# POOL's subtraction of the expert weights cut in four, and a longer allowance for one phase of the routing search

## The chip, the cores and the metric

The kernel runs on one core of a Trainium2 chip. The metric is the device time of one execution in microseconds (us). A core has a matrix engine (PE, TensorE), a vector engine (DVE, VectorE), an activation engine (ACT, ScalarE), a general engine (POOL, GpSimd) and a queue engine (SP) that only issues transfers here. Each engine works through its own list of instructions in order and waits on semaphores for the others.

## The reference

Three layers follow one another, all in float32. Local attention works on chunks of 64 tokens in 8 heads. Its 4608 rows of 512 go through a dense feed-forward layer, `relu(x @ w_in)**2 @ w_out` with 2048 hidden columns. The last layer routes each row to one of 8 experts, and it is the layer of which this document speaks:

```python
logits = x @ w_gate
order = np.argsort(-logits.flatten())
for idx in order:
    tok, e = idx // E, idx % E
    if assigned[tok] >= 0 or counts[e] >= cap:
        continue
    assigned[tok] = e
    counts[e] += 1
...
h = np.maximum(x[mask] @ w1[e], 0.0)
out[mask] = h @ w2[e]
```

Each expert takes exactly `cap` = 576 rows, those that the greedy pass over all 36864 logits gives it.

## The kernel before

**Products.** A float32 matrix is held as a high part, the value rounded to the narrower format that PE multiplies, and a low part, what is left. A product is three matmuls: high by high, high by low, low by high. ACT copies the high part (`WH`, line 920 for expert weights) and another engine subtracts it from the value to get the low part (`WL`, line 921, on POOL, `wl<-raw,wh` in the rows: 128 partitions by 512 columns).

**The greedy pass as a search.** The experts fill up one after another. Phase `ph` (0 to 7) of the search finds the expert that fills next, its threshold and its list of rows. It works on DVE with small matmuls on PE between (`route_phase`). A phase has a start of four steps (lines 700 to 713: `M`, `b`, `wq`, `ch`, `oh`, `mk`), eight rounds that fix four bits of the threshold each, and an end that gives the expert's number (`EID`, line 813) and then the list (`idx`, line 876). A round has a chain from PE to DVE and back: counts on PE (line 733), DVE, a second small matmul (lines 741 and 760 in phases 0 and 1, line 753 from phase 2 on, behind DVE's `c<-all,c` of line 750), DVE's digit and the next thresholds (`thr` line 782, `base` line 784, `mk` line 725, `pre` line 728). Phase 7 has no rounds.

**The experts.** The loop at the end takes the experts `p` = 0 to 7 in the order in which the search finds them. For each of eight slices `f` of the hidden columns it does `up2(p, f)` (192 matmuls in all, line 1007) and, one slice behind, `down2` (112 matmuls, line 1072). Both `down2(p, 6)` and `down2(p, 7)` come at `f` = 7, and between their matmuls PE transposes the five tiles of rows of expert `p+1` (line 985), at places that `SPREAD` fixes. These tiles are fetched by indirect DMAs that POOL issues (`gather`, line 970). They are issued after `up2(p, f)`, as many as are due so that five are done at `f` = 7, but only once the list of `p+1` exists. At `f` = 7 what is missing of the search is put out without delay and what is missing of the five gathers is issued at once. POOL also issues the indirect DMAs that write results (`put`, line 1057).

**What sets the order.** Every engine's list is made by one Python program, with a clock of its own that runs on estimated costs: `tick` adds 0.12 us for a matmul of `up2` and 0.216 us for one of `down2` (192 and 112 of them, 47.2 us an expert). The search is a generator: each `yield` is a step, with the time after which the next step may be put into the lists. `route_step` adds to it the allowance `SLACK`, 0.4 us, under a condition (line 941). Since PE works in order, a small matmul of the search that stands too early makes PE wait for DVE. From phase 2 on a phase has 25 steps and its yields sum to 37.9 us. Phase 1 has 33 steps (four at the start, two in the first round, three in each of seven rounds, six at the end) that sum to 28.2 us. Phase 1 begins in the last stretch of the dense layer, whose right halves of columns are made last (`rest`).

The same clock paces the weights of the experts: `load_expert` starts when `EID` is known, fetches through SP into three buffers, and puts out one unit of 128x512 (16 units an expert) every 2.2 us (1.4 us during expert 0).

Of the kernel before, what the change touches and what calls it, by code (L numbers as in the profile page):

```python
# [7 lines left out]
F32 = mybir.dt.float32  # L8
# [6 lines left out]
OP = mybir.AluOpType  # L15
# [42 lines left out]
def attn_moe_moe2(  # L58
# [12 lines left out]
    nc = tc.nc  # L71
    N, DM = out.shape
# [23 lines left out]
    TAIL = 6  # L96
    TAIL2 = 6
    SLACK = 0.4
    GAPS = 0, 0
    AHEAD = 4  # L100
    Y1 = 2.6, 1.1
# [24 lines left out]
    WH, WL = [None] * NU, [None] * NU  # L126
# [488 lines left out]
    lists = [False] * E  # L615
# [272 lines left out]
    def unit_of(p, n):  # L888

        order = [0]  # L890
        for f in range(1, NFE):
            order += [f, NFE + f - 1]
        order.append(2 * NFE - 1)
        return order[n]

    def load_expert(p):
        base = (p % 2) * NF
        raws = {}
        reg = nc.sync.value_load(EID[p][0:1, 0:1], min_val=0, max_val=E - 1)

        def fetch(n):
            u = unit_of(p, n)
            raw = stg_p.tile([P, 512], F32, tag="raw", name="raw")
            if u < NFE:
                src = w1[bass.ds(reg, 1), u].rearrange("o p z -> p (o z)")
            else:
                f = u - NFE
                src = w2[bass.ds(reg, 1), f * P:(f + 1) * P, :].rearrange("o p d -> p (o d)")
            nc.sync.dma_start(out=raw, in_=src)
            raws[n] = raw  # L910

        for n in range(2):
            fetch(n)
        yield 3.5
        for n in range(2 * NFE):
            if n + 2 < 2 * NFE:
                fetch(n + 2)
            u = unit_of(p, n)
            raw = raws.pop(n)
            nc.scalar.activation(out=WH[base + u], in_=raw, func=AF.Copy)  # L920
            nc.gpsimd.tensor_tensor(out=WL[base + u], in0=raw, in1=WH[base + u].bitcast(F32), op=OP.subtract)  # L921
            have[p] = n + 1
            yield 1.4 if state["cur"] < 1 else 2.2

# [2 lines left out]
    def tick(us):  # L927
        st = state
        st["clk"] += us
        while st["rt"] is not None and st["clk"] >= st["rt_next"]:  # L930
            route_step()
        for p in (st["cur"], st["cur"] + 1):
            if 0 <= p < E and eids[p] and have[p] < 2 * NFE:
                if st["clk"] >= st["ld_next"]:
                    load_step(p)
                break

    def route_step():
        st = state
        try:  # L940
            st["rt_next"] = max(st["clk"], st["rt_next"]) + next(st["rt"]) + (SLACK if sum(lists) > 1 else 0.0)
        except StopIteration:
            st["rt"] = None

    def load_step(p):
        if p not in loaders:
            loaders[p] = load_expert(p)
        try:
            state["ld_next"] = max(state["clk"], state["ld_next"]) + next(loaders[p])
        except StopIteration:  # L950
            have[p] = 2 * NFE

    def need_unit(p, u):
        while not eids[p]:
            route_step()
        n = [unit_of(p, z) for z in range(2 * NFE)].index(u)
        while have[p] <= n:
            load_step(p)
# [3 lines left out]
    def gather(p, cols=None):  # L962

        to = halves[cols.start] if cols else gathered[p]
        s = len(to)
        n = P if s < NS - 1 else LAST
        rows, idx = (x2d, IDX[p]) if cols is None else (x2a, IDX[p]) if cols == LEFT else \
            (x2d.rearrange("n (h c) -> (n h) c", h=2), idx_r)
        xg = xg_p.tile([P, rows.shape[1]], F32, tag=f"x{'a' if cols == LEFT else 'g'}{s}", name="xg")
        nc.gpsimd.indirect_dma_start(  # L970
            out=xg[0:n], out_offset=None, in_=rows,
            in_offset=bass.IndirectOffsetOnAxis(ap=idx[0:n, s:s + 1], axis=0))
        to.append((xg, n))
# [55 lines left out]
    def up_start():  # L1029

        early = ((0, 0, 5), (1, 0, 0), (2, 0, 1), (0, 1, 2), (1, 1, 3))
        pbs = {}
        for cols, chunks in ((LEFT, range(ND // 2)), (RIGHT, range(ND // 2, ND))):
            state["rt_next"] += HOLD[cols == RIGHT]
            for n, (f, z, b) in enumerate(early):
                for s in {0: range(S0), AT: range(S0, NS)}.get(n, ()):
                    xg_T(0, s, chunks)
                if cols == LEFT:
                    if z == 0:
                        up_new(0, f)  # L1040
                    pbs[n] = bank(b, "ph2")
                up_mm(0, f, z, pbs[n], chunks, cols == LEFT, cols == RIGHT)
                if cols == RIGHT:
                    up_out(0, f, z, pbs[n])
            if cols == LEFT:
                for _ in range(GAPS[1]):
                    route_step()
        state["ld_next"] = state["clk"]
        pb = bank(6, "ph2")
        up_mm(0, 2, 1, pb)  # L1050
        up_out(0, 2, 1, pb)
# [39 lines left out]
    with tc.manual_schedule():  # L1091
# [27 lines left out]
        for sl in range(2 * NF + 1, len(order)):  # L1119
# [4 lines left out]
            st, i = f % 4, (2 * TB if j == "c" else (j + 1) * TB) + f // 4  # L1124
# [50 lines left out]
        for _ in range(NS):  # L1175
            gather(0, RIGHT)
        for _ in range(GAPS[0]):
            route_step()
# [84 lines left out]
```

## Time and profile before

| | us |
|---|---|
| median of 3 runs | 1498.09 |
| lowest and highest | 1487.51 and 1498.24 |
| profiled execution, its own time | 1501.74 |
| its span in the trace | 1499.9 |

The span leaves out 1.8 us around the program. The first 960 us are attention and the dense layer, with phase 0 of the search at their end. Phases 1 to 7 and the experts lie between 960 us and 1491 us. A row of a timeline gives the start, the duration, engine, line, operation and tiles, and in brackets the idle time before it and what ended it. Rows of the same instruction that follow one another are merged (x3), and their duration is that of all together.

### The profile page before, as it was taken

The page shows a single profiled execution, that of the slowest core. Times are in us where ns is not written, and L with a number is a line of the kernel's source. Part 1 is how long each engine was busy: PE and PEld are TensorE (multiplying, and loading weights), DVE is VectorE, ACT ScalarE, POOL GpSimd, SP SyncE. Part 2 cuts the span into 40 slices and gives each one's busy share as a digit, 9 for nine tenths or more (in the row PEclk, how much of TensorE's full clock was granted, in tenths as well). Part 3 has the DMA queues.
Part 4 walks back from the last instruction along what each step waited for, and adds up shares of the span by engine and source line. Part 5 has one row for each costly group of instructions (what it writes and reads, how often), then busy time and mean ns, then how long its engine had stood idle before and what let it go on. Part 6 is the DMA issues. An engine that isn't in the chain of part 4 may idle for free.

```text
span 1499.9 us, 25184 instructions
## 1 busy us (share of the span) xinstructions
PE 1409.9 (94%) x9489; PEld 1168.4 (78%) x9489; DVE 1039.0 (69%) x2641; ACT 514.3 (34%) x1133; POOL 311.2 (21%) x269
## 2 busy tenths in 40 slices
PE   3789989999999999999999999988899999899997
PEld 2578878888878888888888877777788887788996
DVE  8999427776777777777777786547787877775121
ACT  4687533323223223232232232123323323233331
POOL 3210000000000100000000001235553645344741
PEclk7799999999999999999999999989999999999999
DMA  6433221201112102021120010214342433423520
GB/s 217 156 128 119 78 70 58 77 29 45 62 36 71 36 29 78 30 78 35 36 78 29 15 43 1 79 59 124 98 127 75 128 99 96 113 73 114 159 81 32
DMA packets 56602, 115.97 MB, mean 77 GB/s; under 512 B 7448, under 2 KB 13080, under 8 KB 56352
## 3 DMA queue, kind: packets, MB, share of 16 engines
q1 hardware_dynamic: 49248, 92.82, 19.8%
q0 software_dynamic: 6112, 20.98, 4.2%
q8 instruction: 75, 1.23, 0.3%
q10 hardware_dynamic: 1120, 0.56, 0.1%
q14 instruction: 47, 0.39, 0.1%
HBM read 90.72 MB, written 23.61 MB: 76 GB/s over the span
## 4 chain that ended last, share of the span: by engine, by line
PE 77%; DVE 17%; ACT 2%; issue 2%; DMA 1%; another core or an unknown queue 0%; SPq 0%; POOLq 0%; DVEq 0%; ACTq 0%
PE acc L482 26%; PE ph L429 23%; PE ph L1007 11%; PE ac L1072 9%; PE ps L308 2%; PE px L382 1%; DVE thr L782 1%; DVE c L750 1%; PE pa L364 1%; PE rp L733 1%; DVE junk L558 1%; DVE s L231 1%; PE pt L985 1%; DVE hl L1019 1%; DVE m L230 1%
## 5 line engine op out<-in xcount | busy, mean ns | idle before, releaser
L921 POOL TENSOR_TENSOR wl<-raw,wh 128x512 fp32r<-128x512 f32 x128 | 164.5, 1298 | 223.6 <-ACT wh L920 209.6
L445 ACT ACTIVATE r<-ph 128x512 f32<-128x512 f32 (+1 forms) x160 | 88.7, 554 | 323.6 <-PE ph L429 314.4
L558 DVE CUSTOM_DVE_ANT_0 junk<-x,wgb 128x512 f16<-128x512 f32 x256 | 178.0, 695 | 4.4
L453 DVE SCALAR_TENSOR_TENSOR r<-ph,r 128x512 f32<-128x512 f32 (+1 forms) x127 | 83.8, 659 | 130.8 <-ACT r L445 130.7
L429 PE MATMUL ph<-xh,wh 128*128 128x512 f32 (+1 forms) x640 | 163.5, 378 | 0.0
L429 PE MATMUL ph<-xh,wl 128*128 128x512 f32 (+1 forms) x640 | 159.1, 370 | 0.0
L429 PE MATMUL ph<-xl,wh 128*128 128x512 f32 (+1 forms) x640 | 158.5, 370 | 0.0
L566 POOL TENSOR_TENSOR wt<-wh,wl 128x512 f32<-128x512 f32 x16 | 25.1, 1572 | 622.3 <-ACT gh L458 366.6
L482 PE MATMUL acc<-wh,gh 128*128 128x512 f32 x512 | 149.7, 409 | 0.0
L482 PE MATMUL acc<-wl,gh 128*128 128x512 f32 x512 | 143.9, 398 | 0.0
L482 PE MATMUL acc<-wh,gl 128*128 128x512 f32 x512 | 142.7, 395 | 0.0
L463 DVE TENSOR_TENSOR gl<-r,gh 128x512 fp32r<-128x512 f32 (+1 forms) x144 | 92.0, 639 | 63.6 <-ACT gh L458 53.2
L429 PEld LDWEIGHTS ph<-xh,wh 128*128 128x128 f32 x640 | 114.3, 190 | 22.6 <-ACT xh L137 0.2
L429 PEld LDWEIGHTS ph<-xh,wl 128*128 128x128 f32 x640 | 114.4, 189 | 21.5
L429 PEld LDWEIGHTS ph<-xl,wh 128*128 128x128 f32 x640 | 114.2, 189 | 21.0
L1017 ACT ACTIVATE hh<-ph 128x256 fp32r<-128x256 f32 x112 | 43.0, 384 | 246.0 <-PE ph L1007 239.1
L482 PEld LDWEIGHTS acc<-wh,gl 128*128 128x128 f32 x512 | 97.0, 189 | 23.1
L482 PEld LDWEIGHTS acc<-wl,gh 128*128 128x128 f32 x512 | 97.2, 190 | 22.3
L458 ACT ACTIVATE gh<-r 128x512 fp32r<-128x512 f32 (+1 forms) x144 | 84.2, 585 | 86.7 <-DVE r L453 83.0
L482 PEld LDWEIGHTS acc<-wh,gh 128*128 128x128 f32 x512 | 90.8, 190 | 19.2
L1007 PE MATMUL ph<-xgh,wh 128*128 128x320 f32 (+1 forms) x512 | 96.1, 306 | 6.1 <-ACT xgh L137 3.7
L1019 DVE SCALAR_TENSOR_TENSOR hl<-ph,hh 128x256 fp32r<-128x256 f32 x112 | 46.9, 421 | 74.4 <-ACT hh L1017 40.2
(227 smaller groups left out, 2620.7 us busy)
## 6 DMA issues: line engine op xcount, KB each, us to landing
raw<-in_moe_w_dram SPq DMA_DIRECT2D x128, 256.0 KB
q<-in_q_dram SPq DMA_DIRECT2D x36, 256.0 KB
k<-in_k_dram SPq DMA_DIRECT2D x36, 256.0 KB
v<-in_v_dram SPq DMA_DIRECT2D x36, 256.0 KB
raw<-in_moe_w_in_dram SPq DMA_DIRECT2D x16, 512.0 KB
raw<-in_moe_w_out_dram SPq DMA_DIRECT2D x16, 512.0 KB
x_rows<-x SPq DMA_DIRECT2D x30, 256.0 KB
x_half<-x SPq DMA_DIRECT2D x30, 128.0 KB
```

The costliest lines, as they stand in the source:

```text
L429: nc.tensor.matmul(ph, lhsT=w[:, a, :], rhs=x[:, a, :], start=(m == 0), stop=(m == 3 * ND - 1))
L445: nc.scalar.activation(out=r, in_=ph, func=AF.Relu)
L453: nc.vector.scalar_tensor_tensor(out=r, in0=ph, scalar=0.0, in1=r, op0=OP.max, op1=OP.mult)
L458: nc.scalar.activation(out=gh, in_=r, func=AF.Copy)
L463: eng.tensor_tensor(out=gl, in0=r, in1=gh.bitcast(F32), op=OP.subtract)
L482: nc.tensor.matmul((acc[j][t] if to is None else to)[:, cols], lhsT=g[:, t * P:(t + 1) * P], rhs=w[:, cols], start=(first and m == 0), sto ...
L558: nc.vector.tensor_tensor_reduce(out=junk, in0=x, in1=late["wgb"][:, e, :], scale=1.0, scalar=0.0, op0=OP.mult, op1=OP.add, accum_out=dst)
L921: nc.gpsimd.tensor_tensor(out=WL[base + u], in0=raw, in1=WH[base + u].bitcast(F32), op=OP.subtract)
L1007: nc.tensor.matmul(pb[:, 0:c1 - c0], lhsT=w[:, a, :], rhs=x[:, a, c0:c1], start=(first and m == 0), stop=(end and m == len(prods) - 1))
L1017: nc.scalar.activation(out=h[:, at:at + b - a], in_=pb[:, a:b], func=AF.Relu)
L1019: nc.vector.scalar_tensor_tensor(out=lo[:, at:at + b - a], in0=pb[:, a:b], scalar=0.0, in1=h[:, at:at + b - a].bitcast(F32), op0=OP.max, o ...
L1072: nc.tensor.matmul(acc2[p][s], lhsT=g[:, s * P:(s + 1) * P] if whole else g, rhs=w, start=(f == 0 and m == 0), stop=(f == NFE - 1 and m == ...
```

## The change

The low part of a unit of expert weights is made by four POOL instructions of 128 columns in place of one of 512. And the allowance of 0.4 us is added to a step as soon as the list of phase 0 exists, and no longer only when the list of phase 1 exists too. So it also holds for the last step of phase 0 and for all steps of phase 1.

```diff
+    PIECE = 128
...
             nc.scalar.activation(out=WH[base + u], in_=raw, func=AF.Copy)
-            nc.gpsimd.tensor_tensor(out=WL[base + u], in0=raw, in1=WH[base + u].bitcast(F32), op=OP.subtract)
+
+            for c in range(0, DM, PIECE):
+                z = slice(c, c + PIECE)
+                nc.gpsimd.tensor_tensor(out=WL[base + u][:, z], in0=raw[:, z], in1=WH[base + u].bitcast(F32)[:, z],
+                                        op=OP.subtract)
             have[p] = n + 1
...
-            st["rt_next"] = max(st["clk"], st["rt_next"]) + next(st["rt"]) + (SLACK if sum(lists) > 1 else 0.0)
+            st["rt_next"] = max(st["clk"], st["rt_next"]) + next(st["rt"]) + (SLACK if lists[0] else 0.0)
```

## Rows read from the trace of the kernel before

**Rows 1.** The page: the engines' busy time, and PE's granted clock in 40 equal slices of 37.5 us, in tenths.

```profile
PE 1409.9 (94%) x9489; PEld 1168.4 (78%) x9489; DVE 1039.0 (69%) x2641; ACT 514.3 (34%) x1133; POOL 311.2 (21%) x269
PEclk7799999999999999999999999989999999999999
```

**Rows 2.** Busy time of the engines by stretch: length, then PE, PEld, DVE, ACT and POOL with their instructions, the granted clock, the DMA share and GB/s. Phase 1 lies in the first two stretches, expert 5 in the third, expert 6 in the fourth.

```profile
960.00:994.00 34.00, 28.11 (x227) 25.51 (x225) 19.62 (x67) 6.92 (x18) 15.04 (x14) 0.90 0.45 135
994.00:1030.00 36.00, 31.33 (x193) 24.30 (x194) 23.18 (x75) 10.09 (x25) 12.70 (x10) 0.81 0.25 74
...
1323.00:1385.00 62.00, 60.15 (x404) 51.61 (x403) 40.70 (x132) 21.06 (x51) 30.84 (x26) 1.00 0.36 107
1385.00:1440.00 55.00, 55.00 (x339) 49.49 (x338) 14.20 (x34) 22.84 (x54) 34.84 (x30) 1.00 0.44 134
```

**Rows 3.** What PE's matmuls waited for between 960 and 1500 us: total us, times, longest.

```profile
PE rp L753 <- DVE c L750: 8.4, 7, 3.2
PE rp L733 <- DVE mk L713: 5.8, 4, 2.2
PE rp L733 <- DVE mk L725: 4.9, 7, 1.4
...
PE rp L857 <- DVE krem L850: 3.1, 1, 3.1
```

**Rows 4.** Short windows: before and behind PE's waits near 970 and 1024 us, and behind those near 1052 and 1305 us. Columns as in rows 2.

```profile
968.00:971.00 3.00, 0.80 (x8) 0.60 (x6) 2.90 (x6) 0.11 (x1) 0.52 (x1) 1.00 0.66 175
971.00:978.00 7.00, 7.00 (x43) 6.49 (x44) 2.65 (x11) 0.00 (x0) 4.86 (x5) 0.51 0.34 95
...
1022.00:1025.70 3.70, 0.63 (x6) 0.39 (x5) 3.49 (x8) 1.85 (x5) 2.85 (x4) 1.00 0.41 106
1025.70:1029.10 3.40, 3.32 (x13) 2.12 (x13) 2.86 (x11) 0.00 (x0) 0.99 (x1) 0.50 0.70 193
...
1053.00:1056.40 3.40, 3.19 (x11) 2.73 (x11) 1.99 (x8) 0.00 (x0) 0.01 (x1) 0.51 0.49 157
...
1305.60:1312.40 6.80, 5.21 (x17) 3.96 (x16) 5.13 (x12) 0.00 (x0) 3.28 (x3) 0.50 0.56 161
```

**Rows 5.** Three DVE groups of the search from 950 us on (count, busy us, mean ns), and the shortest, median and longest ns of the same three lines.

```profile
L750 DVE TENSOR_TENSOR c<-all,c 90x120 f16<-90x120 f16 x40 | 28.2, 706 | 1.4
L782 DVE SCALAR_TENSOR_TENSOR thr<-dg,pre 128x15 int32<-128x15 int32 x37 | 20.8, 563 | 1.3
...
L703 DVE TENSOR_TENSOR b<-b,capA 128x36 f32<-128x36 f32 x6 | 6.1, 1021 | 0.2
...
L750 DVE TENSOR_TENSOR c<-all,c x40: 278/281/4020, 1037.3 to 1352.2; 90x120 f16<-90x120 f16 x40
L782 DVE SCALAR_TENSOR_TENSOR thr<-dg,pre x37: 174/345/3167, 951.0 to 1349.0; 128x15 int32<-128x15 int32 x37
L703 DVE TENSOR_TENSOR b<-b,capA x6: 195/708/3027, 966.6 to 1297.9; 128x36 f32<-128x36 f32 x6
```

**Rows 6.** POOL's groups: the subtraction that is cut, and its shortest kind of instruction that the kernel has with one column.

```profile
L921 POOL TENSOR_TENSOR wl<-raw,wh 128x512 fp32r<-128x512 f32 x128 | 164.5, 1298 | 223.6 <-ACT wh L920 209.6 <-DMA raw<-in_moe_w_dram 12.9
L155 POOL IOTA sgn<- 128x1 int32 x1 | 0.1, 134 | 0.0
```

**Rows 7.** Timeline around 1267 us, POOL and then DVE.

```profile
1264.75 3.79 POOL L921 TENSOR_TENSOR wl<-raw,wh 128x512 fp32r<-128x512 f32 x3
1266.81 0.53 DVE L782 SCALAR_TENSOR_TENSOR thr<-dg,pre 128x15 int32<-128x15 int32 x1
1267.26 1.30 DVE L784 SCALAR_TENSOR_TENSOR base<-dg,base 128x1 int32<-128x1 int32 x1
```

**Rows 8.** Timeline around 1050 us, POOL and then DVE.

```profile
1048.30 0.97 POOL L970 DMA_INDIRECT xg<-x_rows,idx  x1
1049.29 3.71 POOL L921 TENSOR_TENSOR wl<-raw,wh 128x512 fp32r<-128x512 f32 x3
1049.13 4.02 DVE L750 TENSOR_TENSOR c<-all,c 90x120 f16<-90x120 f16 x1
```

**Rows 9.** Timeline: the lists of experts 5 and 6, and PE's first matmul of `down2(4, 6)` and of `down2(5, 6)`, which are the places at `f` = 7.

```profile
1295.13 0.16 DVE L876 SCALAR_TENSOR_TENSOR idx<-jn,rp 128x5 int32<-128x5 f32 x1
1315.32 0.40 PE L1072 MATMUL ac<-wh,hh 128*128 128x512 f32 x1
1365.07 0.16 DVE L876 SCALAR_TENSOR_TENSOR idx<-jn,rp 128x5 int32<-128x5 f32 x1
1376.49 0.40 PE L1072 MATMUL ac<-wh,hh 128*128 128x512 f32 x1
```

**Rows 10.** Timeline: first gathers of expert 6 on POOL, and PE's transposes of its first and last tile. Below, the queue of these DMAs between 1372.4 and 1376.6 us: packets, MB, share.

```profile
1370.57 0.99 POOL L970 DMA_INDIRECT xg<-x_rows,idx  x1
1371.87 0.96 POOL L970 DMA_INDIRECT xg<-x_rows,idx  x1 [0.30 <-issue]
1377.88 0.62 PE L985 MATMUL pt<-ident,xg 128*128 128x128 f32 x4
1383.02 0.46 PE L985 MATMUL pt<-ident,xg 64*128 64x64 f32 x4
...
q0 software_dynamic: 240, 0.79, 64.9%
```

## The prediction

> **What bounds the kernel now.** The page comes first: PE is busy 94% of the span and its clock is full in most slices [rows 1], so time can be won or lost only where PE stands still or is granted the lower clock. The windows by stretch show where the change can act: phase 1 of the search lies in two stretches in which PE has 28.1 of 34 and 31.3 of 36 us of work at a clock of 0.90 and 0.81, while expert 6, beside which nothing is searched, fills 55.0 of 55 us [rows 2]. The waits of PE name the cause: with two smaller lines, PE loses 24 us to DVE's results for the search, 8.4 of them to `c`, 10.7 to `mk` and 3.1 to the end of phase 1 [rows 3]. [...]
>
> DVE is late because POOL holds it up. `c` takes 278 ns and 706 on average, `thr` 174 and 563, `b` 195 and 1021 [rows 5]: 40 x 0.428 + 37 x 0.389 + 6 x 0.826 = 36 us in these three groups. The timeline shows two patterns. At 1266.81 `thr` waits until 1267.34, which is where the second of three POOL subtractions of 1.26 us ends, so DVE is let in between two of them; `base` then waits for the third [rows 7]. At 1049.13 `c` waits 4.02 us, through all three [rows 8]; there an indirect DMA of POOL stands directly before them.
>
> **The change, part by part.** The sum is made against the profiled execution, 1501.74 us, which is 3.65 above the median of the runs, 1498.09.
>
> *Four pieces on POOL.* The price of a 128x128 subtraction is in no row. If nothing of it were fixed it would be 1298/4 = 325 ns; with a fixed part as large as the one-column instruction, 134 ns, it is 134 + 1164/4 = 425 ns [rows 6]. A unit would take 1.3 to 1.7 us; I take 1.6, near the upper end, because a fixed part must exist. 128 units x 0.3 = 39 us more on POOL, which is busy 311 [rows 1]; what hides it is that no matmul waits for `wl` [rows 3]. Without that cover it would cost up to 0.3 us a unit. Behind the pieces POOL's gathers and writes stand up to 0.4 us later.
>
> For DVE a piece is a shorter wait only where it is let in between two instructions. Even there the gain is small for a chain: `thr`, `base` and `mk` follow one another, and if each is let in after one piece, they wait for three pieces, 1.2 us, hardly less than for the rest of one long subtraction. A single `c` gains: its waits without a DMA before them are mostly 0.2 to 1.1 us and would fall below 0.4. Where a DMA stands before the run, DVE waits for the whole run, now 1.6 in place of 1.3 us a unit. Bounds: a gain of 18 us (all of PE's 24 us of waits but the 6 of phase 1) and a loss of 5. I take a gain of 2, nearer to the loss, since the longest waits are of the second kind.
>
> [...]
>
> *The allowance in phase 1.* PE's three waits of this phase are 2.2 us (3.00 less 0.80) at 968 to 971 us, 0.8 at a `mk` and 3.1 at its end [rows 3, 4], 6.1 in all. The half-clock stretches behind the first and the last cost 7.0/2 + 3.4/2 = 5.2. The first wait has four steps of 0.4 before it and the end of phase 0 another: 2.0 us of the planner's clock, which is 2.0 x 62/47.2 = 2.6 us of PE's time [rows 2], so it and its half clock go: 2.2 + 3.5 = 5.7. Of the other 0.8 + 3.1 + 1.7 = 5.6 I take 4, because two steps of 0.4 do not cover three blocked instructions in a row. Gain 9.7; bounds 4 and 11.3.
>
> *What the allowance moves.* Phase 1 has 33 steps: 33 x 0.4 = 13.2 us of the planner's clock, and everything behind it in the search moves. It never catches up, because a later phase needs 37.9 + 25 x 0.4 = 47.9 of that clock and an expert gives 47.2. In PE's time 13.2 is 17.3 us. List 6 now comes at 1365.2 and its last call, `f` = 7 of expert 5, is at 1376.5: 11.3 us ahead. List 5 comes 20 us ahead of its call [rows 9]. Counting the planner's clock through with its own yields, lists 2 to 6 stand 19.8, 17.5, 15.3, 13.0 and 11.2 before their calls, and with the change 6.3, 3.8, 1.7, 0 and 0: for experts 5 and 6 the last one and two steps are put out on the spot with no matmuls between. For experts 3 to 6 all five gathers then go out together at `f` = 7, where now one or two do.
>
> What that costs: a gather moves its rows from 1.9 us after its start (1370.57, packets from 1372.4), 4.2 us for three, so a first tile is there some 3.3 us after, and the next starts come every 1.30 us. PE wants the first tile 1.4 us and the last 6.5 us after the call [rows 9, 10]. Five together are 3.3 + 4 x 1.30 = 8.5 us, so PE is 2.0 us late if the first gather starts at the call. For expert 3 the list is 3.8 x 1.3 = 4.9 us early: nothing. For expert 4 it is 2.2 us early, less 1.5 for the rest of the chain to `idx`: 1.3 late. For expert 5 the last chain is in the way: some 1 us to `idx` and 0.5 of PE's wait, 3.5. For expert 6 two chains: 1.8 and 1.1 more, 4.9. Together 9.7, and the two long waits bring the lower clock, 3.4/2 each as in [rows 4]: 13.1. Bounds: 4, if POOL and PE drift in our favour, and 25, if all four wait and all four lower the clock for 7 us. POOL's queue is in order: behind the gathers the first weights of the next expert stand, 6.5 us; they are wanted some 12 us later, so this costs nothing. SP's fetches start later by the same 17 us with the expert's number, and have the same rate; two units in 4.4 us of the clock against 5.9 us in which PE uses two.
>
> **Sum:** 1501.74 - 2 - 9.7 + 13.1 = 1503.1; less 3.65 for the median, about **1500 us**.
>
> **The rivals.**
> *Faster: DVE is let in after every piece, behind DMAs too.* For it: `thr` was let in after one subtraction [rows 7]; against it: `c` was not [rows 8]. Then three quarters of the 18 us of waits outside phase 1 go, 13.5, and the two half-clock stretches at 1053 and 1306 us [rows 4], (3.4 + 6.8)/2 = 5.1; the other terms stay: 1501.7 - 18.6 - 9.7 + 13.1 - 3.65 = 1483 us. [...]
> *Slower: the late lists.* Place: the call at `f` = 7 of experts 2 to 5. Price: 25 in place of 13.1, with 4 of the 9.7 won in phase 1 and the pieces at +3: 1501.7 + 3 - 4 + 25 - 3.65 = 1522 us. It decides as soon as two calls wait over 5 us each. For it: the lead of 11.3 us against a shift of 17.3; against it: POOL runs ahead of PE when it has no weights to make.
> *The pieces do nothing*: POOL runs them as one, DVE waits as before. That is within my forecast, 2 us above it.
>
> **Chances.** The forecast 0.57, the faster rival 0.20, the slower 0.20, a POOL that itself becomes late with pieces far over 425 ns 0.03. A measurement of this kernel can tell about 1%, 15 us, from no change, since single runs lie 0.7% apart. Half of the faster rival's spread lies beyond 1% and some of the forecast's below: faster 0.20, within 0.58, slower 0.22. The range goes from the faster rival's 1483, less 1 us, to 1518, short of the slower rival's end.
>
> **What would show it.** Phase 1: no wait of PE near 969 us and a full clock until the right halves are done. The list of expert 6 at its call, PE waits at lines 869 and 985 there and five DMA rows in a row on POOL. `c` with a mean near 500 ns and `thr` hardly changed. A piece of 0.33 to 0.43 us. Wrong would be: waits of `c` and `thr` that all end within one piece, or gathers whose tiles are there before PE wants them.

## The result and the profile after

| | before | after |
|---|---|---|
| median of 20 runs each, us | 1497.43 | 1506.28 |
| lowest and highest | 1487.51 and 1502.02 | 1498.01 and 1511.72 |
| profiled execution, its own time | 1501.74 | 1510.38 |
| its span in the trace | 1499.9 | 1508.7 |

The ratio is 1.0062, with a 95% interval of 1.0044 to 1.0079: the change costs 8.9 us. It lies within 1%, which was the likeliest case, and the time lies in the range, 6 us above the forecast.

Lines moved by one to five in the new kernel: 753 is now 754, 985 is 990, 1007 is 1012, and the pieces stand at line 925. Where in the 530 us of the search the time went, windows of both kernels show: busy time of PE, PEld, DVE, ACT and POOL, granted clock, DMA share, GB/s. The kernel before, phase 1 and then phases 2 to 7:

```profile
960.00:1030.00 70.00, 59.45 (x419) 49.81 (x418) 42.80 (x140) 17.01 (x43) 27.74 (x24) 0.85 0.35 104
1030.00:1385.00 355.00, 333.75 (x2229) 285.26 (x2228) 265.75 (x779) 113.89 (x270) 175.48 (x146) 0.99 0.35 104
```

The changed kernel:

```profile
960.00:1030.00 70.00, 67.88 (x527) 58.64 (x526) 40.25 (x150) 22.85 (x57) 44.68 (x85) 1.00 0.39 116
1030.00:1385.00 355.00, 317.92 (x2083) 271.84 (x2082) 242.85 (x753) 101.67 (x244) 196.34 (x368) 0.96 0.31 95
```

A stretch at a clock below full is counted here as losing the missing share of its length. The kernel before shows nearly that: its matmuls of `down2` start 0.43 us apart where the clock is 0.50 (the first two rows) and 0.23 apart at 1.00, so 46% is lost there.

```profile
1054.23 0.63 PE L1072 MATMUL ac<-wh,hl 128*128 128x512 f32 x1
1054.66 0.63 PE L1072 MATMUL ac<-wh,hx 128*128 128x512 f32 x1
...
1077.35 0.39 PE L1072 MATMUL ac<-wh,hl 128*128 128x512 f32 x1
1077.58 0.39 PE L1072 MATMUL ac<-wh,hh 128*128 128x512 f32 x1
```

In phase 1 PE's idle time falls from 10.55 to 2.12 us, and the clock from 0.85 to full is worth 0.15 x 70 = 10.5: a gain of 18.9. Behind it PE's idle time rises from 21.25 to 37.08, and the clock falls by 0.03 x 355 = 10.7: a loss of 26.5. The sum, 7.6, is the 8.8 by which the spans differ, as well as a clock of two digits can give it. So nothing was small here. A large gain was given back, and somewhat more. Both traces lie about 4 us above the median of their kernel, so they can be set side by side.

PE's waits of the changed kernel from 955 us on, which answer to [rows 3] (total us, times, longest):

```profile
PE pt L990 <- DMA xg<-x_rows,idx: 12.8, 5, 4.5
PE rp L754 <- DVE c L751: 7.4, 2, 4.4
PE ph L1012 <- DVE hl L1024: 5.4, 4, 2.6
PE rp L734 <- DVE mk L726: 4.2, 4, 3.5
```

A new line leads: PE waits 12.8 us for the tiles of the next expert. `c` makes PE wait twice in place of seven times, but 4.4 us once. The wait for `krem` at the end of phase 1 is gone, and so is one that [rows 3] leave out, for ACT's `xgh` (the high part of the first expert's rows) at 994 us. In the kernel before, the clock was 0.50 from 995 to 1005 us behind it.

```profile
993.91 0.50 PE L1007 MATMUL ph<-xgh,wh 128*128 128x256 f32 x2 [3.16 <-ACT xgh L137]
```

The calls at `f` = 7 of experts 3 and 5, which gather for experts 4 and 6 (columns as in [rows 7]; list, POOL, PE):

```profile
1240.56 0.16 DVE L877 SCALAR_TENSOR_TENSOR idx<-jn,rp 128x5 int32<-128x5 f32 x1
1238.65 3.75 POOL L925 TENSOR_TENSOR wl<-raw,wh 128x128 fp32r<-128x128 f32 x8 [19.38 <-ACT wh L921]
1242.55 0.99 POOL L975 DMA_INDIRECT xg<-x_rows,idx  x1
1246.50 0.63 PE L990 MATMUL pt<-ident,xg 128*128 128x128 f32 x4 [3.25 <-DMA xg<-x_rows,idx]
...
1378.56 0.29 PE L870 MATMUL rp<-R,o 128*128 128x37 f16 x5 [1.81 <-DVE o L866]
1379.64 0.16 DVE L877 SCALAR_TENSOR_TENSOR idx<-jn,rp 128x5 int32<-128x5 f32 x1
1380.59 0.99 POOL L975 DMA_INDIRECT xg<-x_rows,idx  x1 [1.78 <-issue]
1384.13 0.75 PE L990 MATMUL pt<-ident,xg 128*128 128x128 f32 x4 [3.81 <-DMA xg<-x_rows,idx]
```

For expert 6 the last chain of the search itself stops PE, 1.81 us, and the list comes 1.08 us after that matmul; the tile follows 3.5 us after its gather's start. For expert 4 the list was there (1240.72) 2.5 us before PE wanted the tile (1246.50 less 3.25), but POOL was in eight pieces of weights until 1242.4.

The two longest operations of DVE in the search are those of the second pattern [rows 8], now with pieces (POOL, then DVE, twice):

```profile
1035.63 0.95 POOL L975 DMA_INDIRECT xg<-x_rows,idx  x1 [0.30 <-issue]
1036.59 6.79 POOL L925 TENSOR_TENSOR wl<-raw,wh 128x128 fp32r<-128x128 f32 x16
1037.49 3.81 DVE L751 TENSOR_TENSOR c<-all,c 90x120 f16<-90x120 f16 x1
...
1058.81 1.00 POOL L1062 DMA_INDIRECT out_dram<-o,idx  x1 [1.12 <-DVE ga L765]
1059.83 5.55 POOL L925 TENSOR_TENSOR wl<-raw,wh 128x128 fp32r<-128x128 f32 x12
1059.58 4.86 DVE L785 SCALAR_TENSOR_TENSOR base<-dg,base 128x1 int32<-128x1 int32 x1
```

`base` waits 4.86 us, through eleven of the twelve pieces that follow a DMA without a gap. `c` ends at 1041.30, just behind the eleventh piece of its run (1036.59 + 11 x 0.41 = 1041.1); ACT's copy for the last four pieces ended only at 1041.58, so twelve stood ready. The pieces, `c` and `thr` as groups (count, busy us, mean ns), beside [rows 5, 6]:

```profile
L925 POOL TENSOR_TENSOR wl<-raw,wh 128x128 fp32r<-128x128 f32 x512 | 230.6, 485 | 205.6 <-ACT wh L921 185.6 <-PE rp L860 16.5 <-issue 1.6
...
L751 DVE TENSOR_TENSOR c<-all,c 90x120 f16<-90x120 f16 x40 | 19.0, 474 | 1.4
...
L783 DVE SCALAR_TENSOR_TENSOR thr<-dg,pre 128x15 int32<-128x15 int32 x37 | 14.0, 377 | 1.3
```

### The profile page after: what moved, and what is told of

Same layout as the page of the kernel before. It is cut to its first block, busy times and chain, and to the rows that moved or that the text cites. A ratio compares the mean times of both kernels' runs of the same rounds, so it can differ in the third digit from the quotient of the medians.

```text
span 1508.7 us, 25591 instructions
## 1 busy us (share of the span) xinstructions
PE 1409.4 (93%) x9489; PEld 1168.8 (77%) x9489; DVE 1018.9 (68%) x2641; ACT 515.9 (34%) x1133; POOL 372.9 (25%) x653
## 3 DMA queue, kind: packets, MB, share of 16 engines
q8 instruction: 75, 1.23, 0.3%
## 4 chain that ended last, share of the span: by engine, by line
PE 81%; DVE 12%; DMA 2%; issue 2%; ACT 1%; POOL 1%; SPq 0%; POOLq 0%; DVEq 0%; ACTq 0%
PE acc L483 26%; PE ph L430 23%; PE ac L1077 12%; PE ph L1012 12%; PE ps L309 2%; PE px L383 1%; PE pt L990 1%; DMA xg<-x_rows,idx 1%; PE pa L365 1%; PE rp L734 1%; DVE junk L559 1%; DVE s L232 1%; DVE m L231 1%; PE rest L483 1%; DMA k<-in_k_dram 1%
## 5 line engine op out<-in xcount | busy, mean ns | idle before, releaser
L925 POOL TENSOR_TENSOR wl<-raw,wh 128x128 fp32r<-128x128 f32 x512 | 230.6, 485 | 205.6 <-ACT wh L921 185.6
L1077 PE MATMUL ac<-wh,hh 128*128 128x512 f32 x224 | 94.4, 422 | 0.0
```

The source lines that it names most:

```text
L925: nc.gpsimd.tensor_tensor(out=WL[base + u][:, z], in0=raw[:, z], in1=WH[base + u].bitcast(F32)[:, z], op=OP.subtract)
L1077: nc.tensor.matmul(acc2[p][s], lhsT=g[:, s * P:(s + 1) * P] if whole else g, rhs=w, start=(f == 0 and m == 0), stop=(f == NFE - 1 and m == ...
```

## The experiments

The theory from here: the pieces do nothing, the allowance makes the lists late, and PE waits for the late lists. The first rival: five gathers issued together cost the time, late or not. The second: neither does, and PE waits longer because the search meets POOL's runs at other places.

### One part alone

The first kernel keeps the old allowance and has the four pieces.

```diff
-            nc.gpsimd.tensor_tensor(out=WL[base + u], in0=raw, in1=WH[base + u].bitcast(F32), op=OP.subtract)
+            for c in range(0, DM, PIECE):
...
```

> The four pieces alone, with the allowance of before. Theory A (the pieces help DVE only where no indirect DMA stands before POOL's run, and make the runs behind one longer; the late lists are what costs): within 0.3% of before, ratio 0.997 to 1.003, PE's waits for c, mk and thr about as many us as before (20 to 26), no wait of PE for a gather. Rival B (the pieces are what makes the changed kernel slower): ratio 1.004 or more. Rival C (DVE is let in after every piece everywhere): ratio 0.990 or less, no DVE wait over 0.6 us.

Measured: 1495.11 us, ratio 0.9999 (0.9987 to 1.0010). The pieces are worth nothing in sum, within 2 us. `c` makes PE wait 11.4 us in nine waits, more than the 8.4 before [rows 3]. From 960 to 1030 us PE was busy 64.86 us at a clock of 0.95 (before 59.45 at 0.85), and from there to 1385 us 330.21 at 0.98 (before 333.75 at 0.99): the pieces gain in phase 1 too, and lose behind it.

The second keeps the one subtraction and has the new allowance.

```diff
-... + (SLACK if sum(lists) > 1 else 0.0)
+... + (SLACK if lists[0] else 0.0)
```

> The longer allowance alone, POOL's subtraction in one instruction. Theory A: phase 1 loses its PE waits (6 us and 5 us of half clock), and the five gathers at the last call of experts 3 to 6 cost 12 to 16 us of PE's time and some half clock: ratio 1.003 to 1.008, like the whole change (1.006). Rival B (the pieces are the cost): ratio 0.993 to 1.000. PE waits at the transposes for the gathers: A 11 to 15 us in all.

Measured: 1507.68 us, ratio 1.0075 (1.0059 to 1.0092). All of the loss is the allowance's. Its longest line of PE's waits from 955 us on, somewhat below the 11 to 15 us expected, and its two windows:

```profile
PE pt L985 <- DMA xg<-x_rows,idx: 9.1, 4, 4.5
```

```profile
960.00:1030.00 70.00, 65.84 (x497) 56.27 (x497) 42.58 (x141) 21.55 (x54) 31.41 (x27) 0.98 0.38 111
1030.00:1385.00 355.00, 323.42 (x2144) 276.16 (x2144) 249.01 (x771) 106.78 (x254) 162.40 (x138) 0.98 0.33 98
```

Against the kernel before, phase 1 gains 6.4 us of idle time and 9.1 of clock, and the stretch behind it loses 10.3 and 3.6. This trace is of an execution of 1502.38 us, 5.3 below the median of its kernel, so it shows the gain and too little of the loss.

### Late, or bunched?

The third kernel has the allowance only where phase 1 is hurt first: its four start steps and the last step of phase 0, 2.0 us of the planner's clock in place of 13.2. The lists stay early.

```diff
+        if lists[0] and early[0] < 5:
+            early[0] += 1
+            return SLACK
```

> One subtraction per unit, and the allowance in phase 1 only for its first four steps and the step before them, so that the lists come 2 to 3 us of the planner's clock later and not 13. Theory A: the wait of PE at 969 us and the half clock behind it go, 5.7 us, no gather is waited for: ratio 0.995 to 0.998. Rival (the wait at 969 us only moves into the next round, or PE is ahead of the gathers of the right halves anyway): ratio 0.999 to 1.001.

Measured: 1488.87 us, ratio 0.9951 (0.9934 to 0.9969): faster than both kernels. The two windows of above in it:

```profile
960.00:1030.00 70.00, 62.96 (x475) 53.26 (x475) 48.09 (x149) 19.98 (x50) 32.74 (x28) 0.95 0.39 114
1030.00:1385.00 355.00, 334.69 (x2261) 287.57 (x2260) 261.84 (x778) 115.95 (x276) 177.71 (x150) 1.00 0.36 106
```

Phase 1 gains 3.5 us of idle time and 0.10 x 70 = 7.0 of clock, and nothing is given back behind it. (The traces make the gain look larger than it is: the spans differ by 13.3 us, the ratio by 7.) The wait at 969 us is gone; that at the phase's end is still 2.6 us.

The fourth has the whole allowance in phase 1, and 0.3 in place of 0.4 from phase 2 on, so that the lists, late at first, don't fall behind further.

```diff
+        return SLACK if sum(lists) == 1 else LATER
```

> One subtraction per unit, the longer allowance in phase 1 as in the change, but 0.3 us a step from phase 2 on, so that a later phase takes 45.4 of the planner's clock against the 47.2 of an expert and every list stands 7.7 before its last call. Theory A (the lists' lateness is the cost): no PE wait for a gather, phase 1 as in the change: 8 to 13 us faster than the longer allowance alone, ratio to before 0.992 to 0.998. Rival D (0.1 us less a step gives as much back in waits of PE for the search): ratio 1.000 to 1.006, with 8 us or more of new waits at lines 733 and 753.

Measured: 1498.5 us, ratio 1.0018 (1.0005 to 1.0031). PE's waits for late tiles are gone, and the kernel is 9 us faster than with the same allowance in phase 1 and 0.4 behind it, as the theory said. But the time is in the range of rival D, since the shorter steps let the matmuls of the starts and ends of phases come too early, where the kernel before had 5.8 for the first of these lines [rows 3] and the changed one 1.8 for the second:

```profile
PE rp L734 <- DVE mk L714: 9.9, 4, 2.5
PE rp L870 <- DVE o L866: 7.3, 5, 1.6
```

The fifth is the kernel before, with one condition changed: all five gathers of experts 1 to 6 wait for `f` = 7. It bunches them and delays no list.

```diff
-                if p + 1 < E and f and lists[p + 1]:
+                if p + 2 < E and f == NFE - 1 and lists[p + 1] or p + 2 == E and f and lists[p + 1]:
```

> The kernel before, with its search and its lists in time, but all five gathers of experts 1 to 6 held back to the last call (f = 7); expert 7 as before. It tells the bunching from the lateness. Theory A1 (bunching alone costs, since the first gather starts at the call): 2.0 us of PE's wait at the transposes for each of six experts, 10 to 13 us, ratio 1.006 to 1.010. Theory A2 (what costs is the chain of a late list; with the list there POOL issues the gathers ahead of PE): under 1 us an expert, ratio 0.998 to 1.003.

Measured: 1494.35 us, ratio 0.9962 (0.9950 to 0.9973), faster than before. Bunching is no loss in sum. The trace shows why: for expert 5 POOL starts the first gather 3.4 us before PE starts the `down2` of that place, and the first transpose waits 0.33 us.

```profile
1303.98 0.99 POOL L970 DMA_INDIRECT xg<-x_rows,idx  x1 [0.15 <-issue]
1307.37 0.40 PE L1072 MATMUL ac<-wh,hh 128*128 128x512 f32 x1
1309.39 0.63 PE L985 MATMUL pt<-ident,xg 128*128 128x128 f32 x4 [0.33 <-issue]
```

Of this kernel's waits from 955 us on, those for gathered tiles and for `c`:

```profile
PE pt L985 <- DMA xg<-x_rows,idx: 2.9, 1, 2.9
PE rp L753 <- DVE c L750: 1.9, 5, 0.6
```

One expert of six has a late tile, 2.9 us. PE also waits longer for DVE's low parts of the tiles, 4.7 us in four waits against 1.1 before. But `c` makes PE wait 1.9 us in place of 8.4, and only one of DVE's operations in the search lasts over 3 us, where five did: of the 41 runs of weights between 1030 and some 1247 us 14 stand behind a gather or a write of results, where 23 did.

The sixth adds to the third the five steps before the end of phase 1, to take the wait that is left there.

```diff
+        return SLACK if 1 <= steps[0] <= 5 or 29 <= steps[0] <= 33 else 0.0
```

> As the allowance for the start of phase 1 alone, and also for the five steps before its end, where PE still waits 2.6 us for line 850: the lists come another 2 us of the planner's clock later. If a wait of PE is bought off by the allowance wherever it stands and the lead of the lists is spent only at the end: 2 to 4 us faster than the start alone, ratio to before 0.992 to 0.995. If the lead counts before it is used up (three gathers at f = 6 for experts 4 to 6): ratio 0.996 or more.

Measured: 1505.68 us, ratio 1.0034 (1.0022 to 1.0046). A miss. Its wait at the end of phase 1 is down to 1.4 us and no late tile costs it more than 1.4, and yet it is some 12 us slower than the third, by the ratios (1.0034 less 0.9951, of 1497). In its waits `mk` of line 725 and an `hx` have grown:

```profile
PE rp L733 <- DVE mk L725: 7.0, 9, 1.9
PE ph L1016 <- DVE hx L1028: 3.7, 1, 3.7
```

Behind phase 1 (1030 to 1385 us) PE is idle 27.3 us at a clock of 0.98, where the third kernel has 20.3 at 1.00, and six of DVE's operations in the search last over 3 us, where the third has three. The wait for `hx`, at 1330 us, follows a `thr` of 1.95 and a `base` of 1.28 us beside two subtractions directly behind a write of results. This is what the second rival says: 2 us of the planner's clock move six phases against POOL's work. The seventh kernel has both edits, of the third and of the fifth, and asks whether their gains add.

> The allowance for the last step of phase 0 and the four start steps of phase 1 only, one subtraction of 512, and the gathers of experts 1 to 6 all held to f = 7. If the two gains found singly (ratios 0.9951 and 0.9962) are of different places they add: 0.991, some 1484 us where the kernel before has 1497, with c waits below 3 us in all and no wait at the call above 3 us. Rival: both take away the same waits of c behind DMAs, or the search shifted by 2.6 us lines up with POOL's runs in another way; then no more than the better of the two, 0.995, or nothing, 1.00.

Measured: 1494.89 us, ratio 0.9972 (0.9959 to 0.9984). They don't add. Its waits for `c` fell to 3.7 us, but 5.0 for late tiles came back, 4.0 of them in one.

### When POOL shuts DVE out

Three kernels ask why a wait goes through a whole run of pieces. A small program of its own came first.

> No part of the reference is computed, the output is zeros; eight stages, twice, each with a run of POOL subtractions beside a train of 24 DVE operations with two operands from SBUF. Stages in order: 3 of 512 columns; the same directly behind an indirect DMA; 12 of 128 columns; the same behind an indirect DMA; the same behind an indirect DMA but with a semaphore round through ACT between; 3 of 512 behind a DMA with that round; 1 of 512 behind a DMA; 4 of 128 behind a DMA. Theory A (behind an indirect DMA POOL's run leaves no gap for DVE): in stages 1 and 3 one DVE operation waits for the whole run, 3.5 us and more, in stages 0, 2, 4 and 5 none waits longer than one subtraction, 1.3 or 0.5 us. Rival C (DVE is let in after every subtraction, the long waits of the traces had another cause): no wait over 1.4 us in stage 1, none over 0.6 us in stage 3.

It did not settle it. Twelve pieces behind a DMA let DVE in after 0.40 us, against theory A. In one pass of a stage with a DMA, a DVE operation waited 3.72 us, through all three subtractions; in the other pass of the same stage the longest took 1.21. The gap between the DMA and the run was 0.03 us in the first and 0.10 in the second. The second program sets this gap: the list of the DMA waits for the copy that the subtractions read, so in the direct stages their input is always there first.

```diff
+                V.tensor_reduce(s1, wh.bitcast(F32), AX.X, OP.max)
                 V.tensor_scalar(idx, idx0, 0, None, OP.bitwise_or)
```

> It computes nothing of the reference: its output is zeros. Eight stages, twice each, measure one thing: a run of POOL subtractions behind an indirect DMA, and beside it a train of 24 small DVE operations with two inputs. In stages 0, 4 and 6 the subtraction's input is ready before the DMA, so the run follows it directly (gap 0.02 to 0.03 us); in stages 1 and 5 it comes after the DMA's end, so there is a gap. In stages 2 and 3 a one-column memset or iota of POOL stands between the two, and in stage 7 a memset and a wait for ACT. Theory (DVE is shut out only where the run follows the DMA directly): in stages 0, 4 and 6 a DVE operation that meets the start of the run lasts 3.7 us (three subtractions of 512) or 4.9 us (twelve of 128), in both passes; in stages 1, 5 and 7 each is let in after one subtraction, 1.2 or 0.4 us. Stages 2 and 3 tell whether any instruction between is enough: then 1.2 us, else 3.7. Rival (it is chance, or the lining up of the first DVE operation with the run): direct and late stages show both lengths alike, and in the direct stages not all show the long one.

POOL in two stages of twelve pieces, the first directly behind the DMA, the second 0.39 us behind it:

```profile
124.33 0.98 POOL L78 DMA_INDIRECT xg<-in_v_dram,idx  x1 [5.35 <-DVE idx L77]
125.33 4.98 POOL L96 TENSOR_TENSOR wl<-raw,wh 128x128 fp32r<-128x128 f32 x12
135.57 0.97 POOL L78 DMA_INDIRECT xg<-in_v_dram,idx  x1 [5.26 <-DVE idx L77]
136.93 5.17 POOL L96 TENSOR_TENSOR wl<-raw,wh 128x128 fp32r<-128x128 f32 x12 [0.40 <-ACT wh L84]
```

The 24 DVE operations beside each of the two runs, as shortest, median and longest ns:

```profile
L101 DVE TENSOR_TENSOR r<-a x24: 161/174/4768, 125.2 to 132.5; 128x15 f32<-128x15 f32 x24
...
L101 DVE TENSOR_TENSOR r<-a x24: 159/168/400, 136.4 to 140.8; 128x15 f32<-128x15 f32 x24
```

All four direct stages of 512 columns showed one wait of 3.9 to 4.3 us, all four late ones waits of 1.20 to 1.24 (stage 7 among them), and both passes agree. A memset or an iota between changed nothing: 3.92 to 3.98 us. In this program DVE was let in after one subtraction wherever POOL had waited for ACT between the DMA and the run, 0.32 to 0.40 us, and not with a memset or an iota alone between. The length of the gap doesn't decide: 0.11 us with the iota shut DVE out, 0.10 in the first program didn't.

The last three test this in the kernel. Between an indirect DMA and the next subtraction POOL fetches one number and waits for it, on top of the third kernel's short allowance; then with four pieces; and the pieces without the pause.

```diff
+            nc.gpsimd.dma_start(out=mark, in_=w_gate[0:1, 0:1])
+            nc.gpsimd.memset(mark, 0.0)
```

> The short allowance (last step of phase 0 and four start steps of phase 1), and between an indirect DMA and the next subtraction of expert weights POOL issues a DMA of one number and waits for it, some 2 us, so that no run follows an indirect DMA directly. Theory (only a run directly behind the DMA shuts DVE out for its whole length): no DVE operation of the search waits longer than about 1.3 us any more, PE's waits for c fall from 7.4 us to below 4, and the time is some 5 us below the 1489 of the kernel without the pause, ratio to before 0.991. Rival (DVE is shut out behind any DMA): c waits as before, 0.995. Second rival (POOL has no such 2 us to give: some ten pauses an expert are 20 us of the 62, beside 21 of subtractions and 10 of DMAs): PE waits for wl, slower than 1497.

> As the run before it, with four pieces of 128 columns in place of one of 512. This is the condition of the prediction's faster rival: DVE let in after every piece, behind DMAs too. Theory: waits of DVE of at most 0.45 us, so PE's waits for c and mk fall below 3 us in all, and the time is 3 to 6 us below that of the pause alone: ratio 0.987. Rival (a chain of DVE operations waits for as many pieces as it has links, so a finer cut gives little): as with the pause alone. Second rival: POOL becomes late, 27 us of pieces an expert and 20 of pauses, and PE waits for wl.

> The short allowance and the four pieces, without the pause: what the change would have been with the allowance at the start of phase 1 alone. Theory: the pieces are worth nothing here either, ratio 0.995 as without them, with long waits of DVE directly behind DMAs through ten pieces and more. Rival: pieces and the short allowance add, 0.99; or the pieces shift the search against POOL's runs by chance, 1.00.

Measured: 1497.02 us, ratio 1.0009 (0.9995 to 1.0023), with the pause; 1522.97, ratio 1.0174 (1.0149 to 1.0200), with pieces and the pause; 1494.95, ratio 0.9999 (0.9983 to 1.0015), with pieces alone. So beside the short allowance, which had 0.9951 by itself, the pieces cost some 7 us: seven of DVE's operations in the search last over 3 us, where three did. With the pause no DVE operation of the search lasts longer than 1.77 us, and PE's waits for `c` fall from 7.4 us to 1.1, and yet the kernel is slower than the third. With pieces and pause together DVE is nearly free (count, busy us, mean ns):

```profile
L751 DVE TENSOR_TENSOR c<-all,c 90x120 f16<-90x120 f16 x40 | 13.6, 340 | 1.4
L783 DVE SCALAR_TENSOR_TENSOR thr<-dg,pre 128x15 int32<-128x15 int32 x37 | 8.0, 215 | 1.3
```

`c` is at 340 ns against a shortest of 278, `thr` at 215 against 174 [rows 5]. And this is the slowest kernel of all, with POOL late in its place. The parts of the pause as groups:

```profile
L903 POOL DMA_DIRECT2D mark<-in_moe_w_gate_dram x49 | 28.3, 577 | 0.1
L904 POOL MEMSET mark<- 1x1 f32 x49 | 4.3, 88 | 95.5 <-DMA mark<-in_moe_w_gate_dram 92.7 <-PE ph L1034 2.8
```

The end of one call in the timeline, POOL and then PE:

```profile
1187.52 3.47 POOL L935 TENSOR_TENSOR wl<-raw,wh 128x128 fp32r<-128x128 f32 x8
1191.15 1.33 POOL L996 DMA_INDIRECT xg<-x_rows,idx  x1 [0.15 <-issue]
1194.81 0.66 PE L1012 MATMUL pt<-ident,xg 64*128 64x64 f32 x4 [4.08 <-DMA xg<-x_rows,idx]
```

And PE's waits for gathered tiles from 955 us on:

```profile
PE pt L1012 <- DMA xg<-x_rows,idx: 17.2, 5, 4.1
```

49 pauses cost POOL (28.3 + 4.3 + 95.5)/49 = 2.6 us each, and the gather of the last tile stands behind eight pieces. Of the theory DVE's part holds and the time does not. Of the second rival POOL's lateness holds, but PE waits for gathered tiles and never for `wl`. In both kernels PE also waits for `hl` and `hx`: with the pause alone 3.5 us each at 1401 and 1425, the first of them behind a copy of ACT that had waited 4.0 us for its weights.

## Why the prediction came out right

The forecast was 1500, and 1506.28 was measured, on the side of zero that the sum gave: 1.4 us slower predicted (1503.1 against 1501.74), 8.9 measured. But two of its terms were mis-sized, each beyond its own bounds (9 us too little gain, 13 too little loss), and the errors mostly cancel: that the forecast lies within 6 us is in part luck.

**Four pieces.** Right for this change: a gain of 2 was taken, and 0 measured (0.9999); beside the short allowance it is a loss of 7. That DVE waits through the whole run behind a DMA was read from one row [rows 8]. The changed kernel and the second small program bear it out for all pieces but the last, with a condition that the rows of before didn't name: the run has to follow the DMA directly. The price of a piece was a little low. The records say 485 ns; twelve in a row take 4.98 us, 415 each, while the sixteen at 1036.59 take 424, where 400 was taken and 425 was the bound. `c` fell to a mean of 474 ns, near the 500 of the sign, and nothing waits for `wl`. But `thr`, which was to change hardly, fell from 563 [rows 5] to 377 ns.

**The allowance in phase 1.** Mis-sized: 9.7, with an upper bound of 11.3. The windows show 18.9 for the whole change, idle 8.4 and clock 10.5, and 15.5 with the allowance alone. The term counted three waits, 6.1 us, and two stretches of half clock, 5.2 us [rows 4]. But [rows 2] show 10.6 us of idle time, and a clock of 0.90 over 34 us and 0.81 over 36, together 3.4 + 6.8 = 10.2 us. That half of a stretch at 0.50 is lost was the prediction's estimate; by the starts of `down2`'s matmuls it is 46%. What it left out is above all the wait of 3.2 us for `xgh` at 994 us with the 10.2 us at 0.50 behind it, 5.1 us. It went too, and with it all of the clock's loss.

**What the allowance moves.** Right in its cause, wrong in one step, and mis-sized: 13.1, with bounds of 4 and 25, against 26.5 by the windows. The list of expert 6 comes at its call, with waits at lines 870 and 990 and five DMAs in a row, as was said. For experts 3, 4, 5 and 6 the waits were put at 0, 1.3, 3.5 and 4.9 us. By the waits at the calls they are 1.2, 3.3, 4.5 and 5.6 (1.8 + 3.8): 14.6 in place of 9.7. The step that failed is "PE is 2.0 us late if the first gather starts at the call", which charged the bunching. Without late lists the fifth experiment finds one late tile in six experts, since POOL runs ahead of PE, 3.4 us at expert 5. What PE waits for is the list, and then POOL, which is busy with weights when the list comes (for expert 4 from the list's end at 1240.72 to the gather at 1242.55, 1.8 us). Here the pieces add to it: with the allowance alone POOL was done with its weights, and PE waited 1.9 us for this tile in place of 3.3. The clock behind these waits was put at 3.4. Windows of two stretches behind the calls for experts 5 and 6, and of two behind DVE's waits of 3.81 and 4.86 us:

```profile
1039.80:1046.60 6.80, 5.25 (x17) 4.26 (x17) 4.81 (x13) 2.82 (x7) 6.28 (x14) 0.50 0.53 181
1063.70:1070.50 6.80, 5.38 (x20) 4.18 (x21) 4.43 (x15) 0.00 (x0) 3.63 (x5) 0.50 0.10 39
1312.80:1319.60 6.80, 4.92 (x17) 4.16 (x18) 2.40 (x5) 1.72 (x3) 4.01 (x6) 0.50 0.63 174
1384.50:1387.90 3.40, 3.40 (x13) 2.80 (x12) 0.91 (x2) 1.72 (x3) 3.08 (x6) 0.50 0.71 213
```

At 0.50 the latter two cost (6.8 + 3.4)/2 = 5.1, so the late lists come to 19.7, of which 1.4 lies beyond 1385. The other 8 of the 26.5 have no step in the prediction. Most of it is the clock behind the search's other waits: the first two rows cost 6.8, three more stretches of 3.4 us at 1128, 1200 and 1262 (0.53, 0.53 and 0.52) 4.8, together 11.6 against 5.1 before [rows 4]. Before each of the five, one or two DVE operations had lasted 1.3 to 4.9 us beside POOL's pieces, so by this trace it is the search meeting POOL's runs at other places; no experiment takes that part alone. All these sizes are of one execution: with the allowance alone, in the trace that lies 5 us under its median, the loss behind phase 1 was 13.9.

**The rivals.** The slower one put its point at two calls that wait over 5 us each. One did (5.6 at expert 6, 4.5 at expert 5), and the late lists cost 19.7 of its 25; the larger gain in phase 1 kept the time at 1506. The faster one did not come, as DVE was shut out behind DMAs. Even its condition, once made, was no gain: with pieces and the pause the kernel took 1523, though the pauses' own cost is in that.

Where POOL had waited before its run in the second small program, DVE was let in after one subtraction, as that rival supposed: after 400 ns with pieces and 1.2 us without. Directly behind a DMA it was not: it waited 4.77 us, through eleven pieces of twelve. What keeps it out there isn't shown.

**What stays open.** Why the sixth kernel is 12 us slower than the third isn't shown beyond its waits. Kernels whose search is only placed otherwise came out between 0.995 and 1.003, and no run here lets one say beforehand which.

## What to carry to other kernels

An allowance that saves a wait in one phase moves every later deadline by its sum; give it to the steps whose wait the trace shows, as the third experiment did (0.9951), and count the leads of all later deadlines first. Before cutting an instruction to let another engine in, look for the runs in which it is let in only at the end, and at what stands directly before them. Weigh the clock column over the whole stretch, not only the waits you have looked at, and look for the next engine's lateness behind a wait that you remove: with pieces and the pause PE's waits for `c` were 3.6 us, and those for gathered tiles 17.2.

## What the runs showed of the hardware

A POOL run that follows an indirect DMA within 0.01 to 0.04 us, or with only a one-column memset or iota between (0.05 and 0.11), shut a two-input DVE operation out for 3.7 to 4.9 us where it had three subtractions of 512 columns or twelve of 128 ready. It was let in behind the third of three, but behind the eleventh of twelve; why isn't shown. With a wait of POOL between, 0.32 to 0.40 us for ACT, it was let in after 0.40 us with pieces and 1.2 us without. Back to back a 128x128 subtraction of POOL takes 0.415 us (4.98/12) where a 128x512 one takes 1.23 (3.70/3), so four cost 35% more than one. A one-number DMA that POOL issued and waited for took 2.6 us, the mean of 49 in the kernel with pieces and the pause. And executions of one kernel differ: twenty of the changed kernel took 1498.01 to 1511.72 us, with mean granted clocks between 0.971 and 0.984, and that with the allowance alone had 1502.38 us in its profiled execution and 1507.68 in the median. So one trace's clock is one sample of it.
